# A hand-written order of steps and a table of due times set anew in an attention-then-gated-MLP kernel

## The chip, the cores and the metric

The kernel runs on one core of one Trainium2 chip. The metric is the device time of one execution in microseconds (us). Three runs of the kernel before are shown; an execution taken with the hardware profiler is a further one, and all rows of the trace come from that one.

## The reference

Attention over q, k, v of shape (4 batches, 8 heads, 768 positions, 64) feeds a gated MLP over 3072 tokens. Heads 0, 2 and 6 ("retrieval") see every earlier position; the other five ("streaming") see the first 4 positions and a window of 64.

```python
scores = scale * np.matmul(q, k.transpose(0, 1, 3, 2))
full_mask = causal                                  # retrieval heads
stream_mask = causal & (is_sink | in_win)           # the others
...
a = np.exp(scores - max) / sum
x = np.matmul(a, v)            # -> (3072, 512): a token's 8 heads side by side
h = x @ w_in                   # 512 x 2048
g = h * (1.0 / (1.0 + np.exp(-beta * h)))
out = (g @ w_out).astype(np.float32)                # 2048 x 512
```

## The kernel before

The 3072 tokens are eight chunks of 384 (a batch and one half of its sequence). A chunk has four units, each a pair of heads p and p + 4, so unit u belongs to chunk u // 4. The steps of a unit:

- casts to bf16 of q (`cq`) and k (`ck`), line 286, from a loaded f32 tile `s`; T: six 128 x 128 transposes on TensorE (PE, L371) and two copies out of PSUM, into `KT` (L373) and `QTD` (L377);
- S ("sinks", L354/L355; for one unit of a chunk also `QX`/`KX`, L350/L351): small copies that put the first four keys beside each block; V ("values", L292, L305/L306): v cast into `VX`, and its first rows beside each block in `VO`;
- Q: scores (L473 adds masks, L492 multiplies; L911 for the later chunks) and the exponential on ScalarE (ACT; L500, later L915); P: probabilities times v (L522) and the division (L525, L527); X: transposing the result into `xT` (L554, L556).

The MLP has two kinds of PE step. G1, written m or 1 in the lists below, is four 128 x 128 by 384-column matmuls with `w_in` (L588), a tanh on ACT (L591) and the gate on VectorE (DVE, L594). G2, written s or 2, is four 512-column matmuls with `w_out` (L630); each fourth is followed by an eviction `osb` and a store of 128 tokens (L640). Each chunk needs 16 G1 and 12 G2.

Every engine runs its instructions strictly in the order in which the program issues them (the schedule is manual), and so do the queues that issue transfers: SP for most loads, stores and DMA transposes, the queue of GpSimd (POOL) for `w_in`, `w_out` and the rows of chunks 3 to 7 (L318), ACT for a few. The order is therefore the whole of the tuning, and three tables write it out:

- `RAMP`: a list of tokens for chunks 0 and 1. `cq4p` casts q of unit 4 on POOL (d: DVE, a: ACT). `L10`, `Lv0p` load q/k of chunk 1 or v of chunk 0; a final p or d makes that engine first clear a few columns of the target, and the transfer waits for that. `T4aa` transposes unit 4 with both copies on ACT. `h` clears one column of `w_in_sb` on DVE, `W0` to `W3` load quarters of `w_in` (two transfers each; a G1 with index 0 to 3 needs W0, and so on), `O` loads `w_out` in four transfers. `o0` sets columns of ones, `B` prepares beta, `A1` loads the last third of v of chunk 1.
- `POST`: the tail of that list, with the remaining 24 G1 of chunks 0 and 1, the loads of chunk 2 (`L20` stands in RAMP, `L21d` and `Lv2d` here), its casts `C8`, `C9`, mask copies M, the transfers r of six rows of chunk 3, the transposes T8, T9 and the first four G2 (s).
- `SEQ`: one string for each of 16 groups of scores of chunks 2 to 7, saying which G1, G2 and halves of P (p, q) follow the group; the letters a, b, c are G1 or G2 with another PSUM bank. Beside it stand calls such as `rows_at(at(84), ...)`, `transposes_at`, `v_at`, `sinks_values`: they give a time on the planner's own clock, a running sum of fixed costs per step, at which a transfer or copy is put into its engine's order.

Of the kernel before, what the change touches and what calls it, by code (L numbers as in the profile page):

```python
# [17 lines left out]
def kernel(  # L18
# [14 lines left out]
    B, H, S, D = q.shape  # L33
# [53 lines left out]
    def later(delay, fn):  # L87

        todo = [fn]

        def once():
            if todo:
                todo.pop()()
        heapq.heappush(heap, (clock[0] + delay, count[0], once))
        count[0] += 1
        return once
# [18 lines left out]
    st_u = {}  # L115
# [172 lines left out]
    def cast_v(u, copy=None):  # L288
        b, h2, p = units[u]
        c = u // NPAIR  # L290
        copy = copy or (nc.vector.tensor_copy if 8 <= u < 16 else nc.gpsimd.tensor_copy)
        copy(out=VX[b % 2, p][:, h2 * HT:(h2 + 1) * HT, :, 0:D], in_=staged["v", c][:, :, p:H:NPAIR, :])  # L292

    def values(u, copy=None):

        b, h2, p = units[u]
        ka, kz = (1, 2) if h2 == 0 else (2, 5)
        n = kz - ka
        st_u.setdefault(u, {})["values"] = lambda: None
        cast_v(u, copy)  # L300
        if not streams[p]:
            return
        vx, vo = VX[b % 2, p], VO[b % 2, p]
        h0 = streams[p][0]
        nc.gpsimd.tensor_copy(out=vo[:, ka - 1:kz - 1, :, 0:D], in_=vx[:, ka:kz, h0:2, 0:D])  # L305
        nc.gpsimd.tensor_copy(out=vo[0:n_sink_i, ka - 1:kz - 1, :, 0:D],  # L306
                              in_=vx[0:n_sink_i, 0:1, h0:2, 0:D].to_broadcast([n_sink_i, n, 2 - h0, D]))

    def pos(b, hh):
        return hh ^ (b == B - 1)  # L310

    def load_rows(c):

        b, h2 = chunks[c]

        def one(name, src, t, hh):
            r, w = h2 * HALF + t * 128, pos(b, hh) * D
            nc.gpsimd.dma_start(out=ROWS[c % 2, name][:, t].rearrange("p (a w) -> p a w", a=NPAIR)[:, :, w:w + D],  # L318
                                in_=src[b, hh * NPAIR:(hh + 1) * NPAIR, r:r + 128, :].rearrange("h p d -> p h d"))
        return [lambda n=n, src=src, t=t, hh=hh: one(n, src, t, hh) for n, src in (("k", k), ("q", q)) for t in range(HT) for hh in range(2)]  # L320
# [19 lines left out]
    def sinks_of(u, eng=None):  # L340

        b, h2, p = units[u]
        ka, kz = (1, 2) if h2 == 0 else (2, 5)
        n = kz - ka
        st_u[u]["sinks"] = lambda: None
        if not streams[p]:
            return
        if lent(u):
            here, there = half(pos(b, 0)), half(1 - pos(b, 0))
            nc.gpsimd.tensor_copy(out=QX[u // NPAIR % 2][there, :], in_=st_u[u]["QT"][here, :])  # L350
            nc.gpsimd.tensor_copy(out=KX[b % 2][there, :], in_=KT[b % 2, p][here, 0:128])  # L351
        kt, ko = KT[b % 2, p], KO[b % 2, p]
        eng = eng or (nc.vector if u in (9, 11) else nc.gpsimd)
        eng.tensor_copy(out=ko[:, ka - 1:kz - 1, :], in_=kt[:, ka * 128:kz * 128].rearrange("p (a j) -> p a j", a=n))  # L354
        eng.tensor_copy(out=ko[:, ka - 1:kz - 1, 0:n_sink_i],  # L355
                              in_=kt[:, None, 0:n_sink_i].to_broadcast([128, n, n_sink_i]))
# [299 lines left out]
    h = FO // 2  # L656
# [74 lines left out]
        cast(u, "q")  # L731

    RAMP = """
    cq0p Lv0p ck0d cq1a L10 ck1p T0dd L11p S0p o0 ck2p Q0.m T1da@23 S1d cq2p cq3d Q0 ck3d
    T2ad Q1 T3da B S3d S2p Q2 V0d h W0 V2d P0 Lv1p Q3@6350 V1d V3d cq4p ck4a
    P2 ck5p X0d P1 P3 T4aa S4d cq5d o1 A1 X1a Q4.m Q4 X2d T5da X3d@7 ck6d S5p
    Q5@1603 cq6p W1 m ck7d T6da cq7p m T7da S6d S7d L20p W2 V4d Q6@6102 V6d V5d V7d
    W3 O m P4 Q7@6105 m X4a P5 P7 P6 m X5a m X7a m X6d m
    """

    fills = {}
# [44 lines left out]
        ramp(x)  # L786
    spare[0] = 1
    POST = """
    L21d m M m m m m m R m M m m m Lv2d M m m m m m r m m
    M m m C9 m m C8 m m m s r r T8aa s r r s T9aa s r  # L790
    """
    masks, rows3 = masks_late(1), []

# [36 lines left out]
    def event(kind, delay, fn, behind=()):  # L830

        when = max([clock[0] + delay] + [last_at.get(x, 0.0) + 1 for x in (kind, *behind)])
        last_at[kind] = when
        return later(when - clock[0], fn)

    def rows_at(at, some, gap=1000):
        for i, f in enumerate(some):
            event("rows", at + gap * i, f)

    def transposes_at(at, c, names=("k", "q"), gap=1300):  # L840
        for i, f in enumerate(transposes_dma(c, names)):
            f = event("transposes", at + gap * i, f, ("rows",))
            for u in range(c * NPAIR, (c + 1) * NPAIR):
                st_u[u].setdefault("load", []).append((f, last_at["transposes"]))

    def v_at(at, c, tiles):
        for i in tiles:
            event("v", at + 500 * i, lambda i=i: load_v(c, tiles=[i]))

    def sinks_values(u, at1, at2):  # L850
        s = st_u.setdefault(u, {})
        s["sinks"] = event("sinks", at1, lambda: sinks_of(u), ("transposes",))
        s["values"] = event("values", at2, lambda: values(u), ("v",))

    rows4 = load_rows(4)
# [112 lines left out]
                special[0] = None  # L968

    fresh, late_x = [10, 11], [10, 11]  # L970
    SEQ = ["2cTcTc", "2cqppcq", "2c2ppcppX2Xb1111a", "b22112c", "22c2", "pq121q11p111pp21pp", "ccc2cb12c", "211p1pcq1p1p1p1a2pp11ba", "bc2cca1b121b2", "pp2b211p1p21pp211p1pcc", "abc212c2b2c", "211b222bc", "pq1a1p21p1111pcp1q2p22", "2cb112c1b1a1b12", "2121b12211", "pp22qcpcc", "qpqp2a222c"]
    PVS = {1: [8, 9], 2: [10, 11], 5: [14, 12, 13, 15], 7: [18, 16, 17, 19], 9: [22, 20, 21, 23], 12: [26, 24, 25, 27], 15: [30, 28]}

    def at(us):
        return 1000.0 * us - clock[0]

    for gi in range(ng):
        pvs = PVS.get(gi, [])
        if gi == 0:
            rows_at(0, rows3)  # L980
            transposes_at(800, 3, ("k",), 0)
        if gi == 1:
            st_u[8]["values"]()
            st_u[9]["values"]()
            st_u[10]["values"] = later(1800, lambda: values(10))
            st_u[11]["values"] = later(8000, lambda: values(11))
            rows_at(6600, rows4[0:6], 300)
        if gi == 2:
            rows_at(4300, rows4[6:9], 300)
            transposes_at(500, 3, ("q",), 0)  # L990
            for u in range(12, 16):
                st_u.setdefault(u, {})['sinks'] = event('sinks', 7400, lambda u=u: sinks_of(u), ('transposes',))
        if gi == 3:
            clock[0] = max(clock[0], 75000.0)
            rows_at(at(67), rows4[9:], 1500)
            transposes_at(at(74.5), 4, ("k",))
            transposes_at(at(77.5), 4, ("q",))
            for i, f in enumerate(masks_late(0)):
                later(at(69 + i), f)
        if gi == 4:  # L1000
            v_at(at(83), 4, range(3))
            rows_at(at(84), load_rows(5))
        if gi == 6:
            for i, u in enumerate((18, 16, 17, 19)):
                sinks_values(u, at(87), at(109.5) + 2600 * i)
            transposes_at(at(98), 5, gap=1800)
        if gi == 7:
            v_at(at(103.5), 5, range(3))
            for i, u in enumerate((22, 20, 21, 23)):
                sinks_values(u, at(106.5), at(121) + 800 * i)  # L1010
            rows_at(at(118.5), load_rows(6), 300)
        if gi == 8:
            transposes_at(at(114), 6)
        if gi == 9:
            v_at(at(126), 6, range(3))
            for i, u in enumerate((26, 24, 25, 27)):
                sinks_values(u, at(102.5), at(155) + 3200 * i)
            rows_at(at(143.5), load_rows(7), 700)
        if gi == 10:
            transposes_at(at(147.5), 7)  # L1020
        if gi == 12:
            v_at(at(151), 7, range(3))
            for i, u in enumerate((30, 28, 29, 31)):
                sinks_values(u, at(163), at(150.5) + 1500 * i)
        if gi == 3:
            v_at(0, 3, range(3))
        if gi == 4:
            for i, u in enumerate((14, 12, 13, 15)):
                st_u[u]['values'] = event('values', 0 + 2600 * i, lambda u=u: values(u), ('v',))
        cycle(gi, SEQ[gi], pvs)  # L1030
    cycle(None, SEQ[ng], [u for u in order if last_in[u] == ng - 1])
    while True:
        m = next_m()
# [39 lines left out]
```

## Time and profile before

| | us |
|---|---|
| three runs | 226.93, 229.57, 319.99; median 229.57 |
| profiled execution, its own time | 226.46 |
| its span, first to last instruction | 224.7 |
| PE busy | 216.2 (96%) |
| PE idle in the span | 8.5 |

The profile page gives the busy time of each engine, the span in 40 slices, the chain of work that ended last, and the costliest groups of instructions. Where the text speaks of the timeline it means the instructions of one engine in order of time: start, duration, engine, line, what is written and read, and in brackets how long the engine had been idle and what released it. "issue to landing" is the time of a transfer from its issuing instruction to its data being there.

### The profile page before, as it was taken

The page shows a single profiled execution, that of the slowest core. Times are in us where ns is not written, and L with a number is a line of the kernel's source. Part 1 is how long each engine was busy: PE and PEld are TensorE (multiplying, and loading weights), DVE is VectorE, ACT ScalarE, POOL GpSimd, SP SyncE. Part 2 cuts the span into 40 slices and gives each one's busy share as a digit, 9 for nine tenths or more (in the row PEclk, how much of TensorE's full clock was granted, in tenths as well). Part 3 has the DMA queues.
Part 4 walks back from the last instruction along what each step waited for, and adds up shares of the span by engine and source line. Part 5 has one row for each costly group of instructions (what it writes and reads, how often), then busy time and mean ns, then how long its engine had stood idle before and what let it go on. Part 6 is the DMA issues. An engine that isn't in the chain of part 4 may idle for free.

```text
span 224.7 us, 5312 instructions
## 1 busy us (share of the span) xinstructions
PE 216.2 (96%) x1951; PEld 125.7 (56%) x1951; DVE 140.4 (62%) x364; ACT 154.2 (69%) x308; POOL 101.3 (45%) x227
## 2 busy tenths in 40 slices
PE   7787999999999999999999999999999999999994
PEld 2465766555655557545655565456655556546554
DVE  4776898966877648747957763354963566508700
ACT  2778988869756879467795857675938888238621
POOL 6375766019855848909992089800454000000000
PEclk9999999999999999999999999999999999999999
DMA  6999999999999999997995599917892101321012
GB/s 184 260 290 209 184 231 224 223 178 178 172 160 162 211 102 210 164 186 166 170 158 102 101 207 112 168 64 91 191 96 65 47 3 47 85 82 47 4 47 93
DMA packets 96730, 31.88 MB, mean 142 GB/s; under 512 B 83120, under 2 KB 93760, under 8 KB 96704
## 3 DMA queue, kind: packets, MB, share of 16 engines
q1 hardware_dynamic: 58288, 22.16, 49.1%
q0 software_dynamic: 35968, 8.13, 47.0%
q10 hardware_dynamic: 2448, 1.25, 2.1%
q8 instruction: 15, 0.25, 0.5%
q14 instruction: 11, 0.09, 0.1%
HBM read 27.27 MB, written 6.29 MB: 149 GB/s over the span
## 4 chain that ended last, share of the span: by engine, by line
PE 86%; DMA 8%; DVE 2%; POOL 1%; ACT 1%; issue 0%; ACTq 0%; SPq 0%; DVEq 0%
PE mm L588 37%; PE tp L630 35%; PE po L522 6%; PE sp L911 5%; DMA w_in_sb<-in_moe_w_in_dram 3%; DMA vs<-in_v_dram 3%; DMA s<-in_q_dram 2%; PE tp L615 2%; PE tp L371 1%; DVE es L438 1%; DVE KT L373 0%; PE tp L554 0%; POOL VO L305 0%; PE sp L492 0%; POOL w_in_sb L161 0%
## 5 line engine op out<-in xcount | busy, mean ns | idle before, releaser
L588 PE MATMUL mm<-xT,w_in_sb 128*128 128x384 bf16 x512 | 90.7, 326 | 0.9 <-DMA w_in_sb<-in_moe_w_in_dram 0.8
L594 DVE SCALAR_TENSOR_TENSOR gT<-th,mm 128x384 bf16<-128x384 f32 x128 | 68.4, 551 | 33.0 <-ACT th L591 27.5
L630 PE MATMUL tp<-w_out_sb,gT 128*128 128x512 bf16 x368 | 87.5, 379 | 0.0
L591 ACT ACTIVATE th<-mm,beta_h 128x384 f32<-128x384 f32 x128 | 73.5, 593 | 15.5 <-PE mm L588 10.4
L588 PEld LDWEIGHTS <-w_in_sb 128*128 128x128 bf16 x512 | 48.3, 98 | 33.6 <-issue 1.1
L915 ACT ACTIVATE es<-sp 128x512 bf16<-128x512 f32 (+1 forms) x104 | 49.4, 590 | 8.8 <-PE sp L911 8.8
L630 PEld LDWEIGHTS <-gT 128*128 128x128 bf16 x368 | 34.0, 98 | 35.7 <-DVE gT L594 0.3
L637 ACT ACTIVATE osb<-tp 128x512 f32<-128x512 f32 x20 | 12.0, 598 | 31.3 <-PE tp L630 27.7
L438 DVE TENSOR_TENSOR es<-es,Mh 128x512 bf16<-128x512 bf16 (+3 forms) x62 | 20.2, 366 | 7.7 <-ACT es L915 7.4
L318 POOL DMA_DIRECT2D s<-in_k_dram x30 | 22.4, 760 | 1.8 <-DMA w_out_sb<-in_moe_w_out_dram 1.7
L522 PEld LDWEIGHTS <-es 128*128 128x128 bf16 x472 | 19.2, 97 | 7.0 <-issue 1.2
L318 POOL DMA_DIRECT2D s<-in_q_dram x30 | 22.5, 771 | 0.6 <-issue 0.4
L522 PE MATMUL po<-VX,es 128*128 128x65 bf16 x392 | 20.6, 193 | 0.3 <-DVE w_in_sb L757 0.3
L350 POOL COPY QX<-QTD 64x384 bf16<-64x384 bf16 x4 | 2.0, 504 | 37.9 <-DMA QTD<-s 27.4
L527 DVE TENSOR_TENSOR x<-po,rec 128x384 bf16<-128x384 f32 x32 | 17.8, 558 | 1.3 <-DVE rec L525 0.2
L305 POOL COPY VO<-VX 128x128 bf16<-128x128 bf16 (+3 forms) x24 | 10.1, 419 | 13.0 <-DVE VX L292 7.8
L438 DVE TENSOR_TENSOR es<-es,Mc 128x384 bf16<-128x384 bf16 (+2 forms) x26 | 7.5, 296 | 10.5 <-ACT es L915 10.3
L911 PE MATMUL sp<-QTD,KT 64*128 64x128 bf16 (+2 forms) x245 | 13.9, 230 | 0.0
L500 ACT ACTIVATE es<-sp 128x384 bf16<-128x384 f32 (+1 forms) x32 | 12.0, 462 | 2.7 <-PE sp L492 2.5
L911 PEld LDWEIGHTS <-KT 64*128 64x128 bf16 x245 | 10.2, 94 | 4.7 <-issue 3.8
L354 POOL COPY KO<-KT 128x384 bf16<-128x384 bf16 (+1 forms) x18 | 7.4, 413 | 8.1 <-DMA KT<-s 5.6
L525 DVE RECIPROCAL rec<-po 128x6 f32<-128x6 f32 x32 | 6.1, 192 | 7.9 <-PE po L522 7.7
(79 smaller groups left out, 150.1 us busy)
## 6 DMA issues: line engine op xcount, KB each, us to landing
vs<-in_v_dram SPq DMA_DIRECT2D x23, 256.0 KB, 5.0
out_dram<-osb SPq DMA_DIRECT2D x23, 256.0 KB, 2.3
s<-in_k_dram SPq DMA_DIRECT2D x12, 192.0 KB, 4.8
w_in_sb<-in_moe_w_in_dram POOLq DMA_DIRECT2D x8, 256.0 KB, 7.3
w_out_sb<-in_moe_w_out_dram POOLq DMA_DIRECT2D x4, 512.0 KB, 15.8
s<-in_k_dram POOLq DMA_DIRECT2D x30, 64.0 KB, 5.1
s<-in_q_dram POOLq DMA_DIRECT2D x30, 64.0 KB, 5.0
s<-in_q_dram SPq DMA_DIRECT2D x8, 192.0 KB, 7.6
```

What stands on the lines that cost most here:

```text
L318: nc.gpsimd.dma_start(out=ROWS[c % 2, name][:, t].rearrange("p (a w) -> p a w", a=NPAIR)[:, :, w:w + D], in_=src[b, hh * NPAIR:(hh + 1) * ...
L438: nc.vector.tensor_mul(e, e, m)
L500: nc.scalar.activation(out=es[:, 0:w], in_=got[f][:, 0:w], func=ACTF.Exp, scale=scale)
L522: nc.tensor.matmul(po[:, qi, hh, :], e, val, start=(j == 0), stop=(j == len(lst) - 1))
L527: nc.vector.tensor_mul(x, po[:, :, :, 0:D], rec.to_broadcast([128, HT, 2, D]))
L588: nc.tensor.matmul(hp[:, 0:HALF], w_in_sb[:, mo, fi * 128:(fi + 1) * 128], xT[c][:, mo, :], start=(mo == 0), stop=(mo == MO - 1))
L591: nc.scalar.activation(out=th, in_=hp[:, 0:HALF], func=ACTF.Tanh, scale=beta_h[:, fi:fi + 1])
L594: nc.vector.scalar_tensor_tensor(out=gTs[c][:, fi, :], in0=th, scalar=1.0, in1=hp[:, 0:HALF], op0=ALU.add, op1=ALU.mult)
L630: nc.tensor.matmul(op, gTs[c][:, fi, ns * 128:(ns + 1) * 128], w_out_sb[:, fi, :], start=(fi == 0), stop=(fi == FO - 1))
L637: nc.scalar.activation(out=osb, in_=op, func=ACTF.Copy, scale=0.5)
L911: nc.tensor.matmul(sp[:, a * 128:z * 128], lhs[half(h)], rhs[half(h), q0 * 128:(q0 + z - a) * 128], start=True, stop=True)
L915: nc.scalar.activation(out=es[:, 0:w], in_=sp[:, 0:w], func=ACTF.Exp, scale=scale)
```

## The change

RAMP, POST and SEQ are reordered and most of the due times behind them are changed; no function, no tile size and no arithmetic changes. PE, ACT, DVE, POOL and the SP queue run the same work in another order, except that a few casts and copies change engine: `cq4` from POOL to DVE, `cq5` from DVE to ACT, `ck7` from DVE to POOL, the copy of X1 from ACT to DVE and that of X2 from DVE to ACT.

```diff
     RAMP = """
-    cq0p Lv0p ck0d cq1a L10 ck1p T0dd L11p S0p o0 ck2p Q0.m T1da@23 S1d cq2p cq3d Q0 ck3d
-    T2ad Q1 T3da B S3d S2p Q2 V0d h W0 V2d P0 Lv1p Q3@6350 V1d V3d cq4p ck4a
-    P2 ck5p X0d P1 P3 T4aa S4d cq5d o1 A1 X1a Q4.m Q4 X2d T5da X3d@7 ck6d S5p
-    Q5@1603 cq6p W1 m ck7d T6da cq7p m T7da S6d S7d L20p W2 V4d Q6@6102 V6d V5d V7d
-    W3 O m P4 Q7@6105 m X4a P5 P7 P6 m X5a m X7a m X6d m
+    Lv0p cq0p L10 cq1a o0 ck0d L11p ck1p T0dd S0p Q0.m T1da@23 ck2p S1d cq2p cq3d ck3d Q0
+    T2ad Q1 T3da h S2p B S3d Q2 V0d W0 V2d P0 Lv1p cq4d V1d Q3@6350 V3d ck4a
+    ck5p P2 X0d P1 cq5a P3 X2a T4aa S4d A1 o1 X1d Q4.m Q4 T5da cq6p ck7p X3d@7
+    S5p Q5@1603 ck6d W1 m T6da cq7p m T7da S6p L20p S7d W2 V4d V7d Q6@6102 V6d V5d
+    W3 O m P4 Q7@6105 m X4a P5 m P7 P6 m X5a m X7a X6d m
     """
...
     POST = """
-    L21d m M m m m m m R m M m m m Lv2d M m m m m m r m m
-    M m m C9 m m C8 m m m s r r T8aa s r r s T9aa s r
+    m m m L21d m Lv2d m m m m M m m m M R M m r m r m m m
+    m r m C8 T8aa m m r m m m m r M C9 s s T9aa r s s
     """
...
-    SEQ = ["2cTcTc", "2cqppcq", "2c2ppcppX2Xb1111a", "b22112c", "22c2", "pq121q11p111pp21pp", "ccc2cb12c", "211p1pcq1p1p1p1a2pp11ba", "bc2cca1b121b2", "pp2b211p1p21pp211p1pcc", "abc212c2b2c", "211b222bc", "pq1a1p21p1111pcp1q2p22", "2cb112c1b1a1b12", "2121b12211", "pp22qcpcc", "qpqp2a222c"]
+    SEQ = ["22TcTc", "2cqpqpc", "2c2ppcpqX2Xb1111a", "b2c1122", "2cc", "pqc11q211111qpp21pp", "2c22c21bc", "2111pp1cqp1p1p211pp11ba", "bcccca1b121b2", "pp2b12p112p21p1p1q1cq2", "abc221c2b22", "211b2c2bc", "pq11p2a1p11cp1q1q12p2c", "2cb12c11ba11b12", "2111b2c1c1", "apq2q2pc2", "qppp22c222"]
...
-            transposes_at(800, 3, ("k",), 0)
+            transposes_at(300, 3, ("k",), 0)
-            rows_at(4300, rows4[6:9], 300)
-            transposes_at(500, 3, ("q",), 0)
+            rows_at(1800, rows4[6:9], 500)
+            transposes_at(300, 3, ("q",), 0)
...
-            transposes_at(at(77.5), 4, ("q",))
+            transposes_at(at(80.5), 4, ("q",))
-            rows_at(at(84), load_rows(5))
+            rows_at(at(82.5), load_rows(5))
-                sinks_values(u, at(87), at(109.5) + 2600 * i)
-            transposes_at(at(98), 5, gap=1800)
+                sinks_values(u, at(86.5), at(115.5) + 2100 * i)
+            transposes_at(at(99.5), 5, gap=1800)
...
-            transposes_at(at(147.5), 7)
+            transposes_at(at(149), 7)
-            v_at(at(151), 7, range(3))
+            v_at(at(153.5), 7, range(3))
-                sinks_values(u, at(163), at(150.5) + 1500 * i)
+                sinks_values(u, at(162), at(150.5) + 2600 * i)
-                st_u[u]['values'] = event('values', 0 + 2600 * i, lambda u=u: values(u), ('v',))
+                st_u[u]['values'] = event('values', 0 + 300 * i, lambda u=u: values(u), ('v',))
```

In the built program, some moves show that the lists don't tell. The sinks of chunk 7 (QX, KX, KO on POOL), which stood before most of its values, stand behind all of them. On SP, the store of one `osb` moves from before the three `KT` transposes of chunk 7 to between the second and the third, and the first v transfer of chunk 5 moves ahead of that chunk's three `QTD` transposes.

More of the change, by code (lines that the diff above doesn't have):

```diff
@@ L984 @@
             st_u[9]["values"]()
-            st_u[10]["values"] = later(1800, lambda: values(10))
+            st_u[10]["values"] = later(500, lambda: values(10))
             st_u[11]["values"] = later(8000, lambda: values(11))
@@ L988 @@
         if gi == 2:
-            rows_at(4300, rows4[6:9], 300)
-            transposes_at(500, 3, ("q",), 0)
+            rows_at(1800, rows4[6:9], 500)
+            transposes_at(300, 3, ("q",), 0)
             for u in range(12, 16):
-                st_u.setdefault(u, {})['sinks'] = event('sinks', 7400, lambda u=u: sinks_of(u), ('transposes',))
+                st_u.setdefault(u, {})['sinks'] = event('sinks', 3600, lambda u=u: sinks_of(u), ('transposes',))
         if gi == 3:
             clock[0] = max(clock[0], 75000.0)
-            rows_at(at(67), rows4[9:], 1500)
+            rows_at(at(67), rows4[9:], 3000)
             transposes_at(at(74.5), 4, ("k",))
-            transposes_at(at(77.5), 4, ("q",))
+            transposes_at(at(80.5), 4, ("q",))
             for i, f in enumerate(masks_late(0)):
@@ L1001 @@
             v_at(at(83), 4, range(3))
-            rows_at(at(84), load_rows(5))
+            rows_at(at(82.5), load_rows(5))
         if gi == 6:
             for i, u in enumerate((18, 16, 17, 19)):
-                sinks_values(u, at(87), at(109.5) + 2600 * i)
-            transposes_at(at(98), 5, gap=1800)
+                sinks_values(u, at(86.5), at(115.5) + 2100 * i)
+            transposes_at(at(99.5), 5, gap=1800)
         if gi == 7:
-            v_at(at(103.5), 5, range(3))
+            v_at(at(104.5), 5, range(3))
             for i, u in enumerate((22, 20, 21, 23)):
-                sinks_values(u, at(106.5), at(121) + 800 * i)
-            rows_at(at(118.5), load_rows(6), 300)
+                sinks_values(u, at(107.5), at(116) + 300 * i)
+            rows_at(at(119.5), load_rows(6), 300)
         if gi == 8:
-            transposes_at(at(114), 6)
+            transposes_at(at(113.5), 6)
         if gi == 9:
-            v_at(at(126), 6, range(3))
+            v_at(at(127.5), 6, range(3))
             for i, u in enumerate((26, 24, 25, 27)):
-                sinks_values(u, at(102.5), at(155) + 3200 * i)
-            rows_at(at(143.5), load_rows(7), 700)
+                sinks_values(u, at(105.5), at(156.5) + 1300 * i)
+            rows_at(at(139.5), load_rows(7), 300)
         if gi == 10:
-            transposes_at(at(147.5), 7)
+            transposes_at(at(149), 7)
         if gi == 12:
-            v_at(at(151), 7, range(3))
+            v_at(at(153.5), 7, range(3))
             for i, u in enumerate((30, 28, 29, 31)):
-                sinks_values(u, at(163), at(150.5) + 1500 * i)
+                sinks_values(u, at(162), at(150.5) + 2600 * i)
         if gi == 3:
```

## Prediction

> **What bounds the kernel now.** I read the page first.
>
> ```profile
> PE 216.2 (96%) x1951; PEld 125.7 (56%) x1951; DVE 140.4 (62%) x364; ACT 154.2 (69%) x308; POOL 101.3 (45%) x227
> ```
>
> PE is busy for all but 8.5 of the span's 224.7 us, and the change adds and removes no PE instruction. So the question is where these 8.5 us lie, which the busy times by stretch answer (columns: stretch, its length, then PE busy with its count, weight loads, DVE, ACT, POOL).
>
> ```profile
> 1.30:22.00 20.70, 16.73 (x192) 9.78 (x193) 14.04 (x44) 14.30 (x35) 12.18 (x50) 1.00 1.12 253
> 22.00:31.15 9.15, 9.05 (x123) 6.46 (x121) 7.79 (x22) 8.09 (x20) 7.58 (x18) 1.00 1.11 202
> 31.15:48.00 16.85, 16.85 (x104) 10.07 (x103) 15.45 (x37) 14.84 (x26) 4.36 (x7) 1.00 1.21 216
> 75.00:190.00 115.00, 114.98 (x1032) 65.64 (x1031) 70.39 (x177) 83.11 (x164) 57.04 (x114) 1.00 1.02 126
> 221.90:224.70 2.80, 0.00 (x0) 0.00 (x0) 0.00 (x0) 0.23 (x1) 0.00 (x0) 1.00 0.16 47
> ```
>
> Before 22 us PE idles 20.70 - 16.73 = 3.97 us; from there to 31 us 0.10; in the 115 us from 75 to 190 0.02. The end, 2.8 us, is the last eviction and store, which the change does not touch, and 1.3 us pass before the first instruction. The granted clock is 1.00 throughout. So there is nothing to win behind 31 us and at most 4.1 us ahead of it; behind 31 us every new wait is a loss. The chain of waits says what set the start:
>
> ```profile
> 5.79 0.43 SPq L151
> ...
> 12.50 0.32 POOL VO L305
> ...
> 13.86 7.39 DMA w_in_sb<-in_moe_w_in_dram
> 21.25 0.14 issue
> 21.39 0.81 PE mm L588 x4
> ```
>
> The second of three v transfers of chunk 0 is issued at 5.79; when v is there it is cast on DVE and copied on POOL (12.50); behind that copy W0 is issued, its second half lands at 13.86 + 7.39 = 21.25, and the first G1 starts at 21.39. The PE timeline shows what PE did meanwhile, and that it then waited:
>
> ```profile
> 20.37 0.23 PE L492 MATMUL sp<-QTD,KT 64*128 64x128 bf16 x2
> 21.39 0.81 PE L588 MATMUL mm<-xT,w_in_sb 128*128 128x384 bf16 x4 [0.79 <-DMA w_in_sb<-in_moe_w_in_dram]
> ```
>
> 0.79 us is thus the wait that an earlier W0 can remove, while everything PE has left before it (up to the scores Q5, ending at 20.6) isn't slower.
>
> **The change, part by part.** *Lv0p to the front.* The rows of POOL, then those of DVE:
>
> ```profile
> 4.65 0.50 POOL L286 CAST qkb<-s 128x384 bf16<-128x384 f32 x1 [0.20 <-DMA s<-in_q_dram]
> 5.10 0.11 POOL L148 MEMSET vs<- 128x3 f32 x1
> ```
>
> ```profile
> 12.07 0.64 DVE L292 CAST VX<-vs 128x384 bf16<-128x384 f32 x2 [0.52 <-DMA vs<-in_v_dram]
> 12.38 0.06 DVE L757 MEMSET w_in_sb<- 128x1 bf16 x1
> ...
> 13.63 0.56 DVE L527 TENSOR_TENSOR x<-po,rec 128x384 bf16<-128x384 f32 x1
> 14.11 0.83 DVE L292 CAST VX<-vs 128x384 bf16<-128x384 f32 x2
> ```
>
> The clearing of `vs` at 5.10 no longer stands behind the cast cq0, so the first of three v transfers is issued up to 0.5 us earlier. But the second is issued at 5.79, by the chain as an earlier load lands, which the change leaves alone, and the last decides. Bounds: 0 (the second holds) to 0.5 us earlier (all three move); I take 0, as the chain's row shows the second one waiting. *h ahead of V0:* the VO copy at 12.50 starts when h ends (12.38 + 0.06); without h between, when V0's cast ends, about 12.07 + 0.64/2 = 12.39. Gain 0.05: W0 lands at 21.2.
>
> *cq4 on DVE.* The cast takes 0.55 us (quoted below) between x of unit 0, ending at 14.2, and V1, V3 at 14.11, pushing these and what follows back by 0.5. V1 feeds P1 and P3; their cover, POOL's VO copies, ends about when PE needs them, so PE reaches T4 some 0.2 us later (an estimate from these rows), which the next step's longer delay contains. *X2 before T4, and cq5 and X2's copy on ACT.* The rows of ACT:
>
> ```profile
> 15.50 0.54 ACT L286 CAST qkb<-s 128x384 bf16<-128x384 f32 x1
> 16.57 0.48 ACT L373 COPY KT<-tp 128x384 bf16<-128x384 bf16 x1 [0.53 <-PE tp L371]
> ...
> 18.19 1.53 ACT L500 ACTIVATE es<-sp 128x384 bf16<-128x384 f32 x4 [0.24 <-PE sp L492]
> 19.58 0.51 ACT L377 COPY QTD<-tp 128x384 bf16<-128x384 bf16 x1
> ```
>
> ACT had 0.53 us idle before T4's copy at 16.57. Now cq5 (another 0.54, from 16.04 to 16.55) and X2's copy (0.48, to 17.05) stand there, so T4's copies start about 0.5 later, Q4's exponentials at 18.7 instead of 18.19, and T5's copy, on which Q5 waits, at 20.1 instead of 19.58. Q5 then ends at 21.1 instead of 20.6. What covers this is the 0.79 us wait for W0; X2's three transposes, taken earlier, fill PE while it waits for T4's copies. So the first G1 starts at the later of 21.2 (W0) and 21.1 (Q5): 0.1 to 0.2 us earlier than 21.39, and the wait shrinks to 0.1. Were ACT's lag 0.8 us, the first G1 would be later than before by what exceeds it. *The rest of RAMP* (ck7 on POOL while it idled, V7 before V6, S6, which copies nothing, one m between P5 and P7) moves work within the stretch 22 to 31.15, where PE idles 0.10 us: 0.
>
> *POST.* T8 moves from behind the first G2 into the run of G1, C9 out of it.
>
> ```profile
> 48.42 0.34 PE tp L371 x6
> ```
>
> ```profile
> 48.63 0.48 ACT L373 COPY KT<-tp 128x384 bf16<-128x384 bf16 x1 [0.45 <-PE tp L371]
> 49.00 0.48 ACT L377 COPY QTD<-tp 128x384 bf16<-128x384 bf16 x1
> ```
>
> In that run, 31.15 to 48.00, ACT is busy 14.84 of 16.85 us and PE all of it. T8 brings 0.85 us of ACT work (48.63 to 49.48) against 0.34 of PE: ACT falls 0.5 us behind, which the free banks of `mm` may hide. Bounds 0 and 0.5; I take 0.1, as DVE, which sheds the cast of C9 (0.55), was at 15.45 of 16.85 there without stopping PE. *Lv2d and L21d.* A G1 takes 0.65 us (the 104 matmuls of that stretch are 26 G1 in 16.85 us). v of chunk 2 stands six G1 earlier in the list, 3.9 us, and L21 three later, 2 us; beside them runs the last `w_out` transfer:
>
> ```profile
> w_out_sb<-in_moe_w_out_dram POOLq DMA_DIRECT2D x1, 512.0 KB, 19.9
> ```
>
> ```profile
> 27.88 3.01 POOL L165 DMA_DIRECT2D w_out_sb<-in_moe_w_out_dram  x4
> ```
>
> ```profile
> 50.66 1.03 PE L630 MATMUL tp<-w_out_sb,gT 128*128 128x512 bf16 x4
> ```
>
> The fourth is issued at 27.88 + 3 x 0.75 = 30.1 and lands 19.9 later, at 50.0; the G2 that reads it runs at 50.66. Cover 0.65 us. In that stretch SP's queue has loads outstanding anyway, so I take 0; if not, below.
>
> *SEQ and due times.* The same G1 and G2 stand between the scores in each group to within one step, so they come where they came. What changes is how early the small copies are ready. The case that loses most cover is chunk 7; two stretches of POOL, its sinks and the last of its values, and the scores that read them:
>
> ```profile
> 159.90:162.90 3.00, 3.00 (x28) 1.91 (x27) 2.78 (x8) 2.49 (x6) 2.73 (x9) 1.00 1.06 246
> 166.60:171.60 5.00, 5.00 (x38) 2.54 (x37) 0.69 (x2) 3.33 (x8) 4.59 (x10) 1.00 0.33 92
> ```
>
> ```profile
> 180.14 0.22 PE L911 MATMUL sp<-QX,KX 64*128 64x128 bf16 x1
> ```
>
> Chunk 7's sinks ran in the first stretch (nine instructions, 2.73 us busy in 3.00). Now they stand behind the values, which end at 171.6: 171.6 + 3.0 = 174.6, with 180.14 - 174.6 = 5.5 us of cover. Charged 0; the 0.02 us of the long stretch bounds a gain, nothing bounds a loss.
>
> Sum against the profiled execution, 226.46: -0.15 + 0.1 = -0.05, so **226.4**. The median of the three runs, 229.57, is 3.1 us above that execution and the lowest run 0.5; two of four executions lie within 0.5 us, so I forecast on the profiled one.
>
> One rule speaks against the change.
>
> ```profile
> L286 POOL CAST qkb<-s x10: 499/504/537, 4.7 to 34.0; 128x384 bf16<-128x384 f32 x10
> ```
>
> ```profile
> L286 DVE CAST qkb<-s x6: 542/548/553, 4.3 to 20.3; 128x384 bf16<-128x384 f32 x6
> ```
>
> The DVE cast now falls at 14.1 to 14.7, over W0's second issue (13.86 to 14.5). If one blocked the other, W0 would land 0.55 later, at 21.8, and the first G1 start 0.4 later than before: 226.46 + 0.4 + 0.1 = 227.0. The POOL casts, some beside DVE's, spread over 38 ns, which speaks against it. The Trainium skill, SBUF — State Buffer, section "SBUF: two separate sides", has such a rule: an f32 copy on DVE inside SBUF can take the port pair that GpSimd needs to write its transfers' descriptors, and the later one waits for the whole instruction. By it the sum would be 227.0; the trace, as far as these casts show, doesn't agree.
>
> **The rivals.** (1) *The start gains more:* v lands 0.5 earlier and ACT keeps up; PE loses all of the 0.79 wait. 226.46 - 0.8 = 225.7. For it: the earlier first v transfer. Against: the row at 5.79. (2) *DVE blocks POOL,* or T8's ACT work shows in full: 227.0, as above. (3) *w_out lands late.* If v of chunk 2, 3.9 us earlier on the other queue, takes half the engines for those 3.9 us, the fourth `w_out` lands 1.95 us later and the G2 at 50.66 waits 1.95 - 0.65 = 1.3: 226.46 + 1.3 = 227.8. For it: cover of 0.65 only. Against: SP's queue is loaded either way. The Trainium skill, DMA: Bandwidth & Descriptors, section "Queues, rings and completion order", says each engine alternates between the queues that have work, packet by packet; by that rule the half above is the share. (4) *Slower:* the v transfers of chunk 7 stand on SP behind the store now between its KT transposes; that store waits for its `osb`. If they slip by more than 5.5 us, sinks and PE at 180.14 slip by the excess; from 10 us on the kernel is 4.5 us slower, about 231. For it: nothing in the trace bounds that store. Against: its G2 moves by a step or two, under 1 us each. (5) *The change doesn't act at all* where it is meant to: PE's Q5 becomes the bound as W0 did; that is inside the forecast.
>
> **How the numbers follow.** Forecast, 226.4 ± 0.6 us, 0.54; (1) 0.14; (2) 0.08; (3) 0.08; (4) and the like in other groups 0.11; a gain over 4.5 us, which would need more than the 4.1 us of idle, so that instructions now stretched by waits would have to shorten too, 0.05. Two per cent, 4.5 us, is about what a measurement of this kernel can tell from no change. Only (4) is slower by that: faster 0.05, same 0.84, slower 0.11. The range: 225.3 takes in (1); above, the forecast, (2), (3) and the scatter by which the shown median lies 3 us over its own profiled execution: 229.4.
>
> **What would show it.** The wait of the first G1 for `w_in` falls from 0.79 to under 0.3 while that G1 still starts at 21.1 to 21.4; ACT's exponentials of Q4 start near 18.7; PE is again without gaps from 31 to 221.9 us. Wrong would be: an idle row over 0.5 us on PE behind 31 us, at the fourth G2 (rival 3) or at scores of chunk 7 (rival 4), or a first G1 before 20.8 (rival 1).

## The result and the profile after

| | before | after |
|---|---|---|
| median of 22 runs each, side by side | 227.06 | 228.00 |
| lowest | 225.89 | 227.08 |
| profiled execution, its own time | 226.46 | 228.09 |
| its span | 224.7 | 226.4 |

The ratio after to before is 1.0047, with a 95% interval of 1.0027 to 1.0067: the changed kernel is slower by about 1.07 us (0.0047 x 227.06). A few runs in which the chip was in a slower state are left out of it, so it differs a little from the ratio of the medians above. The loss is far inside two per cent, and the time lies in the range given; but it is a loss where a change of -0.05 us was forecast, and it can be told from none.

First, where along the span the loss arises. The chain of waits lists PE's work in order of time (start, duration, what); the scores at L911 and the last transposes at L615 stand in both kernels and serve as milestones. The kernel before:

```profile
51.68 0.66 PE sp L911 x13
...
125.00 0.67 PE sp L911 x20
...
147.27 0.82 PE sp L911 x19
...
218.28 3.55 PE tp L615 x48
```

The kernel after:

```profile
52.07 0.66 PE sp L911 x13
...
125.44 0.67 PE sp L911 x20
...
148.90 0.82 PE sp L911 x19
...
219.90 3.55 PE tp L615 x48
```

After minus before: 0.39 at the first scores of chunk 2, 0.44 at 125 us, 1.63 at 148.9, 1.62 at the end. So in these two executions there are two steps, about 0.4 us lost before 52 us and 1.2 us lost between 125 and 149, and everything else costs nothing that shows. The list of waits on PE (who waited for whom, us in total, times, longest) names the second at once, in the kernel after:

```profile
PE mm L588 <- DMA xT<-x: 1.0, 1, 1.0
```

That line is not in the list of before, while the wait of L588 for `w_in`, 0.8 us there, is gone. PE's timeline of the kernel after shows which G1 it is:

```profile
142.79 0.65 PE L588 MATMUL mm<-xT,w_in_sb 128*128 128x384 bf16 x3
144.47 0.32 PE L588 MATMUL mm<-xT,w_in_sb 128*128 128x384 bf16 x1 [1.03 <-DMA xT<-x]
```

In the kernel before, the same G1 runs without a gap:

```profile
141.49 0.81 PE L588 MATMUL mm<-xT,w_in_sb 128*128 128x384 bf16 x4
```

A G1 has four matmuls, one for each unit's slice of `xT`. This is the first G1 of chunk 5: in the kernel after three slices are there, the fourth, that of unit 23, is 1.03 us late. The SP queue tells why. Before:

```profile
133.06 5.01 SPq L538 DMA_TRANSPOSE xT<-x  x3
138.31 0.40 SPq L640 DMA_DIRECT2D out_dram<-osb  x1
```

After, with the row of ScalarE that the store waits for:

```profile
134.31 3.14 SPq L538 DMA_TRANSPOSE xT<-x  x2
138.75 0.36 SPq L640 DMA_DIRECT2D out_dram<-osb  x1
139.20 1.21 SPq L538 DMA_TRANSPOSE xT<-x  x1
```

```profile
138.13 0.60 ACT L637 ACTIVATE osb<-tp 128x512 f32<-128x512 f32 x1 [1.33 <-PE tp L630]
```

Before, the last transpose of the chunk stood ahead of the store. After, the store of an `osb` stands ahead of it, and the store waits for its eviction, which ends at 138.13 + 0.60 = 138.73. This swap is one more move on the SP queue beside the two that the section on the change names. The chain of waits walks the same way:

```profile
138.13 0.60 ACT osb L637
...
139.20 5.23 DMA xT<-x
...
144.47 0.32 PE mm L588
```

x of unit 23 was there at 138.09 (its division on DVE runs from 137.53 for 0.56), so the store held the transpose from 138.1 to 139.2, 1.1 us. The transpose takes 5.23 us to land, and PE pays 1.03 of it. (The new order also makes that x 1.2 us later than before, where it was there at 136.87, and the G1 1.3 us later; experiment 1 shows what this alone does.) In the kernel before there was hardly any cover to lose, cover being the time from the landing of the data to its being read. Its last transpose, on SP:

```profile
136.90 1.18 SPq L538 DMA_TRANSPOSE xT<-x  x1
```

It landed 5.0 us after its issue, at 141.9, and the fourth slice was read at about 142.0: a cover of about 0.1 us.

The first step, 0.4 us, lies in RAMP. PE's timeline there, after:

```profile
20.24 0.43 PE L473 MATMUL sp<-Ns,idb 128*128 128x384 bf16 x2 [0.26 <-ACT es L500]
...
21.17 0.81 PE L588 MATMUL mm<-xT,w_in_sb 128*128 128x384 bf16 x4
22.24 0.49 PE L371 MATMUL tp<-idb,qkb 128*128 128x128 bf16 x6 [0.26 <-ACT es L500]
```

The first G1 waits for nothing and starts 0.22 us earlier than before (21.39). But behind it T6, which needs the PSUM bank of Q5's scores, now waits for ACT's exponentials of Q5, which it didn't before, so the lead is lost: T6 comes 0.21 us later. A second new wait ends the stretch:

```profile
31.36 0.34 PE L554 MATMUL tp<-idb,x 128*128 128x128 bf16 x3 [0.24 <-DVE x L527]
31.53 0.65 PE L588 MATMUL mm<-xT,w_in_sb 128*128 128x384 bf16 x3
```

The rows of T6 and of the run of G1 in the kernel before, neither with a wait:

```profile
22.03 0.50 PE L371 MATMUL tp<-idb,qkb 128*128 128x128 bf16 x6
...
31.15 1.14 PE L588 MATMUL mm<-xT,w_in_sb 128*128 128x384 bf16 x6
```

The run of G1 starts at 31.53 against 31.15 before. X6 waits for the last division on DVE. DVE's timeline, after and then before, shows a gate (L594) that has come between the two last divisions (L527):

```profile
29.58 0.56 DVE L527 TENSOR_TENSOR x<-po,rec 128x384 bf16<-128x384 f32 x1
30.05 0.54 DVE L594 SCALAR_TENSOR_TENSOR gT<-th,mm 128x384 bf16<-128x384 f32 x1
...
30.74 0.56 DVE L527 TENSOR_TENSOR x<-po,rec 128x384 bf16<-128x384 f32 x1
```

```profile
29.38 0.56 DVE L527 TENSOR_TENSOR x<-po,rec 128x384 bf16<-128x384 f32 x1
...
30.08 0.56 DVE L527 TENSOR_TENSOR x<-po,rec 128x384 bf16<-128x384 f32 x1
```

It is the gate of the G1 that RAMP moved between P5 and P7; the division comes 0.66 us later.

### The profile page after: what moved, and what is told of

The parts are those of the page before. It is cut to its first block, busy times and chain, and to the rows that moved or that the text cites. A ratio compares the mean times of both kernels' runs of the same rounds, so it can differ in the third digit from the quotient of the medians.

```text
span 226.4 us, 5286 instructions
## 1 busy us (share of the span) xinstructions
PE 215.3 (95%) x1929; PEld 125.8 (56%) x1951; DVE 140.9 (62%) x363; ACT 154.1 (68%) x309; POOL 100.8 (45%) x227
## 3 DMA queue, kind: packets, MB, share of 16 engines
q1 hardware_dynamic: 58288, 22.16, 49.8%
## 4 chain that ended last, share of the span: by engine, by line
PE 82%; DMA 7%; DVE 4%; ACT 2%; issue 2%; POOL 1%; ACTq 0%; SPq 0%; DVEq 0%; POOLq 0%
PE mm L588 35%; PE tp L630 33%; PE po L522 6%; PE sp L911 5%; DMA vs<-in_v_dram 3%; DMA xT<-x 2%; DMA s<-in_q_dram 2%; PE tp L615 2%; ACT es L500 1%; DVE x L527 1%; PE tp L371 1%; POOL VO L305 1%; PE sp L492 1%; PE sp L473 1%; DVE gT L594 1%
## 5 line engine op out<-in xcount | busy, mean ns | idle before, releaser
L588 PE MATMUL mm<-xT,w_in_sb 128*128 128x384 bf16 x512 | 90.8, 326 | 1.2 <-DMA xT<-x 1.0
L594 DVE SCALAR_TENSOR_TENSOR gT<-th,mm 128x384 bf16<-128x384 f32 x128 | 68.4, 551 | 36.7 <-ACT th L591 31.0
L591 ACT ACTIVATE th<-mm,beta_h 128x384 f32<-128x384 f32 x128 | 73.4, 594 | 18.7 <-PE mm L588 13.7
L630 PE MATMUL tp<-w_out_sb,gT 128*128 128x512 bf16 x346 | 84.1, 379 | 1.4 <-issue 0.3
L588 PEld LDWEIGHTS <-w_in_sb 128*128 128x128 bf16 x512 | 48.2, 98 | 32.5 <-DVE x L527 0.5
L438 DVE TENSOR_TENSOR es<-es,Mh 128x512 bf16<-128x512 bf16 (+3 forms) x62 | 20.7, 374 | 6.2 <-ACT es L915 5.9
L527 DVE TENSOR_TENSOR x<-po,rec 128x384 bf16<-128x384 f32 x32 | 17.8, 557 | 1.1
L305 POOL COPY VO<-VX 128x128 bf16<-128x128 bf16 (+3 forms) x24 | 9.6, 399 | 15.5 <-DVE VX L292 14.8
L292 POOL CAST VX<-vs 128x384 bf16<-128x384 f32 x16 | 8.1, 526 | 18.2 <-DMA vs<-in_v_dram 18.2
L438 DVE TENSOR_TENSOR es<-es,Mc 128x384 bf16<-128x384 bf16 (+2 forms) x26 | 8.3, 324 | 11.3 <-ACT es L915 11.2
L911 PE MATMUL sp<-QTD,KT 64*128 64x128 bf16 (+2 forms) x245 | 13.9, 230 | 0.0
L911 PEld LDWEIGHTS <-KT 64*128 64x128 bf16 x245 | 10.2, 94 | 5.1 <-issue 4.6
```

Source lines behind the costliest of these rows:

```text
L438: nc.vector.tensor_mul(e, e, m)
L527: nc.vector.tensor_mul(x, po[:, :, :, 0:D], rec.to_broadcast([128, HT, 2, D]))
L588: nc.tensor.matmul(hp[:, 0:HALF], w_in_sb[:, mo, fi * 128:(fi + 1) * 128], xT[c][:, mo, :], start=(mo == 0), stop=(mo == MO - 1))
L591: nc.scalar.activation(out=th, in_=hp[:, 0:HALF], func=ACTF.Tanh, scale=beta_h[:, fi:fi + 1])
L594: nc.vector.scalar_tensor_tensor(out=gTs[c][:, fi, :], in0=th, scalar=1.0, in1=hp[:, 0:HALF], op0=ALU.add, op1=ALU.mult)
L630: nc.tensor.matmul(op, gTs[c][:, fi, ns * 128:(ns + 1) * 128], w_out_sb[:, fi, :], start=(fi == 0), stop=(fi == FO - 1))
```

## The experiments

The theory after reading the profile: the loss is the transpose behind the store (about 1.2 us in the profile) plus ACT's and DVE's lag in the new RAMP (about 0.4). The main rival: a loss in transfers that the profiled execution happens not to show, or in other parts of the order. Ten kernels ran, each with 6 to 12 timed runs beside the kernel before on the same chip; every ratio is to that. Experiments 1 to 4, 5 to 8, and 9 and 10 ran on three chips, and a ratio has an interval of about 0.2% to each side, so a difference of two ratios is uncertain by some 0.3%, 0.6 us. The position of the scores of chunk 2 is that of the first instruction at L911 in the chain of waits, 51.68 before and 52.07 after.

**1. Transpose first.** The kernel after, with the fourth transpose of chunk 5 put into SP's order without delay, so that it stands ahead of the store:

```diff
-                        later(700, lambda: x_by_dma(u))
+                        later(0 if u == 23 else 700, lambda: x_by_dma(u))
```

> The changed kernel with one edit: the fourth xT transpose of chunk 5 is issued on SP ahead of the store that stood before it. If the store is what made it late (theory), it is issued at 138.1, when its x is ready, instead of 139.2, lands near 143.3, the wait of 1.03 us at the G1 that reads it falls under 0.2, the span falls by 1.0 to 1.2 us to about 225.3, and the ratio to the kernel before goes from 1.0047 to 1.000 +- 0.002. If the later place of the last P in the ninth string is what made it late (rival), the transpose still goes out after 138.7, the wait stays over 0.6 and the ratio over 1.003. If something later takes the place of the wait (second rival), the wait goes but the ratio stays over 1.003.

Measured: 226.91, ratio 1.0021 (1.0002 to 1.0040), span 225.1. SP and PE in this kernel:

```profile
133.86 5.35 SPq L538 DMA_TRANSPOSE xT<-x  x3
139.30 0.54 SPq L640 DMA_DIRECT2D out_dram<-osb  x1
```

```profile
142.71 0.81 PE L588 MATMUL mm<-xT,w_in_sb 128*128 128x384 bf16 x4
```

All four slices are read without a gap; the wait is gone, and the span is 1.3 us shorter than after's. Of the 0.47% some 0.26% are gone, and 0.21% are left: a little more than was expected, as the 0.4 us of RAMP had not been counted there. The transpose was issued at 138.03 and landed after 4.4 us, at 142.4; the fourth slice was read at 143.2. So the later x alone, the rival, left 0.8 us of cover: it is the store in front that made the wait.

**2. Store first, in the kernel before.** The opposite edit: the same transpose is delayed until it stands behind the store.

```diff
-                        later(700, lambda: x_by_dma(u))
+                        later(1800 if u == 23 else 700, lambda: x_by_dma(u))
```

> The kernel before with the reverse edit alone: the fourth xT transpose of chunk 5 goes behind the store that followed it. Theory: that store waits for its osb until 138.3, the transpose is issued at 138.75 instead of 136.9 and lands near 143.8; the G1 that reads it wanted it at 142.0: a wait of 1.8 us, ratio to before 1.008 (1.006 to 1.009). Rival (stores and transposes on SP pass without cost, the loss has another cause): no wait, ratio 1.000 +- 0.002.

Measured: 228.47, ratio 1.0079 (1.0055 to 1.0102), span 226.6. The SP queue and the G1 of this kernel:

```profile
138.07 0.36 SPq L640 DMA_DIRECT2D out_dram<-osb  x1
138.51 1.21 SPq L538 DMA_TRANSPOSE xT<-x  x1
```

```profile
143.84 0.32 PE L588 MATMUL mm<-xT,w_in_sb 128*128 128x384 bf16 x1 [1.94 <-DMA xT<-x]
```

One swap of two entries in one queue makes the kernel before slower than the whole change does. Here the G1 comes at 141.25, earlier than in the kernel after (142.79), so it waits longer, 1.94 us, and 0.0079 x 226.69 = 1.8 us of it show in the time; about as expected (1.8 us, 1.006 to 1.009). With the first experiment this settles the cause of the second step from both sides.

**3. Old RAMP and POST in the kernel after.**

> The changed kernel with RAMP and POST of before; SEQ and due times stay new. Theory: the 0.4 us by which the changed kernel reaches the scores of chunk 2 later comes from the new RAMP and goes with it, the 1.0 to 1.2 us at the transpose stay: first scores of chunk 2 at 51.7 instead of 52.07, ratio to before 1.005 +- 0.002, so 0.4 us under the changed kernel. Rival (the ramp's shift is recovered behind, as the transposes and casts of chunk 2 are then waited for): no difference from the changed kernel. If the new SEQ needs the new POST (second rival), new idle rows appear between 48 and 64 us and it is slower than the changed kernel.

Measured: 227.22, ratio 1.0025 (1.0004 to 1.0045), span 226.0. PE waits 1.36 us for `xT` at chunk 5, and the scores of chunk 2 come at 51.42, so the 0.4 us are gone and the other step stays. The ratio lies just under the 1.003 to 1.007 that were expected.

**4. New RAMP and POST in the kernel before.**

> The kernel before with RAMP and POST of the changed kernel; SEQ and due times stay old. Theory: only the ramp's 0.4 us: scores of chunk 2 at 52.05 instead of 51.68, no wait at the G1 of chunk 5, ratio 1.002 (1.000 to 1.003). Rival (new ramp and store interact: an earlier or later arrival decides the wait at the transpose): the wait of 1 us appears here too, ratio 1.005 or more.

Measured: 227.28, ratio 1.0019 (0.9999 to 1.0039), span 225.3; scores of chunk 2 at 52.13, no wait for `xT`. In PE's timeline of this kernel both waits of the new RAMP stand again:

```profile
22.30 0.49 PE L371 MATMUL tp<-idb,qkb 128*128 128x128 bf16 x6 [0.41 <-ACT es L500]
...
31.41 0.34 PE L554 MATMUL tp<-idb,x 128*128 128x128 bf16 x3 [0.25 <-DVE x L527]
```

The two halves add up: 0.19% (experiment 4) and 0.25% (experiment 3) make 0.44%, and the change costs 0.47%, each with 0.2% to both sides. The interval of the RAMP half alone touches 1, so by these times alone it isn't certain. The lowest runs speak for it: 226.66 here and 226.54 in experiment 1, with the new RAMP, against 225.91 for the kernel before beside them (29 runs). The next experiments look at it.

**5. ACT's load put back.** Experiment 1, with cq5, X1 and X2 at the place and on the engine that they had before.

```diff
-    ck5p P2 X0d P1 cq5a P3 X2a T4aa S4d A1 o1 X1d Q4.m Q4 T5da cq6p ck7p X3d@7
+    ck5p P2 X0d P1 P3 T4aa S4d cq5d A1 o1 X1a Q4.m Q4 X2d T5da cq6p ck7p X3d@7
```

> The changed kernel with the transpose first (as in the first experiment) and, in RAMP, X2, X1 and cq5 where and on the engines where they stood before. Theory: X2's copy and cq5 on ACT put T4's copies and the exponentials of Q4 and Q5 0.5 us back, and T6, whose PSUM bank Q5 holds, waits for them (0.41 us in the first experiment); with them back, exponentials of Q4 start at 18.1 instead of 18.65, T6's wait is under 0.1, scores of chunk 2 start 0.3 to 0.5 earlier, near 51.65 instead of 52.05, ratio to before 1.000 +- 0.002. Rival (w_in's landing again sets the pace): the wait moves to the first G1, which then starts no earlier than 21.0, T6 right behind it, and the gain is under 0.2.

Measured: 226.31, ratio 0.9989 (0.9972 to 1.0005), span 224.7, scores of chunk 2 at 51.66. PE's timeline:

```profile
21.18 0.81 PE L588 MATMUL mm<-xT,w_in_sb 128*128 128x384 bf16 x4 [0.64 <-DMA w_in_sb<-in_moe_w_in_dram]
21.82 0.50 PE L371 MATMUL tp<-idb,qkb 128*128 128x128 bf16 x6
22.16 0.81 PE L588 MATMUL mm<-xT,w_in_sb 128*128 128x384 bf16 x4
```

The first G1 starts when it did in the kernel after, at 21.18, though now it waits 0.64 us for `w_in` again; but T6 behind it waits for nobody, and the second G1 starts at 22.16 instead of 22.57. So the rival came in its first half, the wait at the first G1, and not in its second: the scores of chunk 2 come 0.39 us earlier than in experiment 1 (52.05). The two ratios (1.0021 there) differ by 0.3%, or 0.7 us, which the intervals allow to be anything from 0.1 to 0.6%. So taking back what cq5, X1 and X2 did together is enough to remove the RAMP step, and nothing that shows is left of the loss. X6's wait is still there (0.25 us); it uses up the 0.21 us by which the second G1 is ahead of the kernel before (22.37).

**6. The G1 between P5 and P7 put back.** Experiment 1, with that G1 behind X7 as before.

```diff
-    W3 O m P4 Q7@6105 m X4a P5 m P7 P6 m X5a m X7a X6d m
+    W3 O m P4 Q7@6105 m X4a P5 P7 P6 m X5a m X7a m X6d m
```

> The changed kernel with the transpose first and, in RAMP, only the G1 that moved between P5 and P7 put back behind X7. Theory: its gate stands on DVE ahead of the division of the last unit, so X6 waits for x (0.25 us in the first experiment); put back, that wait goes and scores of chunk 2 start 0.2 earlier, near 51.85. Rival (X6 waits because everything on DVE is late by ACT's lag): the wait stays and nothing moves.

Measured: 226.68, ratio 1.0031 (0.9998 to 1.0063). In the profile X6's wait is gone, T6's 0.42 us stays, and the scores of chunk 2 come 0.17 us earlier than in experiment 1. The times can't show 0.17 us (0.08%) with an interval of 0.65%; the price of this edit rests on the profile alone.

**7. Both.**

> The two last edits together. Theory: they add, scores of chunk 2 at 51.4 +- 0.15, span 224.5, ratio to before 0.999 to 1.000; what is left of the new RAMP (v's clearing first, h first, cq4 on DVE, ck7 on POOL) is worth 0 to 0.2 us to the good. Rival (what is left costs by itself, cq4 on DVE above all): scores of chunk 2 at 51.7 or later.

Measured: 226.15, ratio 1.0001 (0.9979 to 1.0023). The time is that of experiment 5, but the profiled execution (226.78, slower than its median) missed the mark: scores of chunk 2 at 52.03 and not 51.4. Its PE timeline has another new wait:

```profile
25.19 0.43 PE L522 MATMUL po<-VX,es 128*128 128x65 bf16 x9 [0.25 <-DVE VX L292]
```

and its chain of waits leads back to a transfer of v of chunk 1:

```profile
14.53 10.05 DMA vs<-in_v_dram
```

In this execution that v took 10 us, and P4 had to wait for its cast. Nothing in the two edits changes that transfer's place in its queue. But 51.7 or later was also the sign of the rival, that the rest of the new RAMP costs something by itself, so this profile doesn't refute it; the times speak against it (1.0001, lowest run 225.85).

**8. Only the front in the kernel before.** v of chunk 0 first, o0 and the second load of chunk 1 ahead of ck1, and `h` ahead of V0:

```diff
-    cq0p Lv0p ck0d cq1a L10 ck1p T0dd L11p S0p o0 ck2p Q0.m T1da@23 S1d cq2p cq3d Q0 ck3d
-    T2ad Q1 T3da B S3d S2p Q2 V0d h W0 V2d P0 Lv1p Q3@6350 V1d V3d cq4p ck4a
+    Lv0p cq0p L10 cq1a o0 ck0d L11p ck1p T0dd S0p ck2p Q0.m T1da@23 S1d cq2p cq3d Q0 ck3d
+    T2ad Q1 T3da h B S3d S2p Q2 V0d W0 V2d P0 Lv1p Q3@6350 V1d V3d cq4p ck4a
```

> The kernel before with only the first part of the new RAMP: v's clearing first on POOL, the ones and the clearing for the next load ahead of ck1, h ahead of V0. Theory: W0 is issued at 12.9 instead of 13.12 and lands 0.1 to 0.3 earlier; first G1 at 20.8 to 21.2, scores of chunk 2 at 51.2 to 51.5, ratio 0.999 +- 0.002: too little to tell from no change by time. Rival (the first v transfer, issued earlier, holds up q and k of units 2 and 3): T2 and T3 later than 7.9 and 10.2 and no gain at the first G1.

Measured: 226.15, ratio 0.9998 (0.9971 to 1.0026). PE's timeline:

```profile
20.56 0.82 PE L588 MATMUL mm<-xT,w_in_sb 128*128 128x384 bf16 x4
21.80 0.49 PE L371 MATMUL tp<-idb,qkb 128*128 128x128 bf16 x6 [0.41 <-ACT es L500]
```

The first G1 starts 0.83 us earlier than in the kernel before and waits for nothing. Little of that is the edit's: W0 was issued at 13.07 against 13.12, and not at 12.9 as expected, but its two transfers landed after 6.2 us (median) against 7.0. Yet the gain is 0.2 us at T6 (21.80 against 22.03) and none in the time: where `w_in` doesn't hold PE, ACT's exponentials do, 0.41 us of it at the next step.

**9. Old RAMP, new SEQ, transpose first.** The last cell of the square: experiment 3 with the edit of experiment 1.

> RAMP and POST of before, everything else as after, with the fourth xT transpose of chunk 5 ahead of the store: the last cell of the square of old and new RAMP by old and new SEQ. Theory (the whole loss is the transpose behind its store plus ACT's and DVE's lag in the new RAMP; the rest of SEQ and of the due times is worth nothing): no wait for xT at chunk 5, first scores of chunk 2 at 51.4 to 51.7, span 224.4 to 224.8, ratio to before 0.997 to 1.001. Rival A (the rest of SEQ costs something of its own): PE idle rows behind 52 us, ratio 1.002 or more. Rival B (SEQ gains once the two faults are out): ratio below 0.997.

Measured: 226.12, ratio 0.9989 (0.9969 to 1.0009). In its profile PE doesn't wait for `xT`, and no wait over 0.2 us stands behind 52 us. So SEQ and the due times, with the one transpose in its place, neither cost nor bring anything that shows, that is, more than 0.3%. The profiled execution was the slowest of its twelve runs, 227.37 with a span of 225.7, and missed the positions that were expected: scores of chunk 2 at 52.6. Its timeline says what was late in this execution, `w_in` at the first G1 and the v of chunk 1 behind `VO` (15.19 to 25.17 in its chain of waits, as late as in experiment 7):

```profile
21.96 0.81 PE L588 MATMUL mm<-xT,w_in_sb 128*128 128x384 bf16 x4 [1.32 <-DMA w_in_sb<-in_moe_w_in_dram]
...
26.44 0.19 PE L522 MATMUL po<-VO,es 128*128 128x65 bf16 x1 [0.23 <-POOL VO L306]
```

**10. The same with the front of experiment 8.**

> The kernel of the run before in this list, with v of chunk 0 loaded first and the clearing of w_in ahead of V0 as well, the only part of the new RAMP that shortens a wait. Theory: first G1 at 20.6 without a wait for w_in, T6 then waits 0.4 for ACT, scores of chunk 2 at 51.4, span 224.4, ratio 0.996 to 1.000: no gain beyond the noise, as ACT takes back what W0 gives. Rival (w_in's landing is what scatters the time from run to run, so that the runs close up and the median falls): ratio 0.994 to 0.997, spread of the runs under 0.5 us.

Measured: 226.19, ratio 0.9980 (0.9957 to 1.0003), runs from 225.90 to 226.70, span 224.3. No version ran that is faster than the kernel before beyond its interval; this one comes nearest. The first G1 starts at 20.85, still 0.39 us behind `w_in`, so the wait didn't vanish as expected, and the runs spread over 0.8 us where the rival asked for less than 0.5.

## Why the prediction was wrong

*The start, up to the first G1: right, step by step.* ACT's exponentials of Q4 were to start at 18.7, T5's copy at 20.1, the first G1 at 21.1 to 21.2 with its wait for `w_in` nearly gone. ACT's timeline of the kernel after:

```profile
18.65 1.53 ACT L500 ACTIVATE es<-sp 128x384 bf16<-128x384 f32 x4 [0.61 <-PE sp L492]
20.04 0.51 ACT L377 COPY QTD<-tp 128x384 bf16<-128x384 bf16 x1
```

and the G1 stands at 21.17 without a wait, bound by PE's own scores Q5, as rival 5 said; rival 1, a first G1 before 20.8, did not come. Two things in it are luck. W0 was issued 0.21 us earlier (12.91 against 13.12) where 0.05 had been charged. And the 21.39 of before is one execution: with the same RAMP the first G1 stood anywhere from 20.90 to 21.96 (last section), so that a gain of 0.15 us could not have been told from the scatter.

*The gain of 0.15 us, carried to the end, and "The rest of RAMP ...: 0": wrong, 0.4 us.* In the profiles the 0.22 us gained at the first G1 were 0.20 us lost at the second G1 (22.57 against 22.37, T6's wait) and 0.38 us lost at 31.53 (X6's wait, from the m between P5 and P7). The first of these steps followed ACT's lag to the first G1 and stopped there, as if a lag ended at the milestone for which it had been worked out. The wait for `w_in` had been covering ACT for T6 too; once PE no longer waited, ACT's exponentials of Q5 became the next bound. That PE idled only 0.10 us in that stretch bounded what could be gained there and said nothing of what could be lost; for SEQ the prediction said so itself, and for RAMP it took the same number for a reason to charge nothing.

*"So they come where they came", charged 0: the step that failed most, 1.2 us in the profile and 0.6 to 0.8 us by the times of experiments 1, 3 and 9.* It looked for the cover of the readers by groups of scores and checked one case, the sinks of chunk 7, with 5.5 us. The case with the least cover was another: `xT` of the last unit of a chunk, read about 0.1 us after it had landed. The prediction asked what is queued behind a waiting store once, in chunk 7 (rival 4), and not for the store that came ahead of a transpose of chunk 5 on the same queue. It named the right sign of it, an idle row over 0.5 us on PE behind 31 us, though at neither of the places that it had in mind; the row of 1.03 us is that. That the measured time still lies in the range is luck: its upper end, 229.4, was set for rivals 2 and 3 and for scatter, and none of these made the loss.

*POST, v and w_out of chunk 2 (rival 3): as forecast.* From 31.5 to 52 us the lag stays at 0.38 to 0.39 us, so T8's work on ACT cost nothing where 0.1 had been charged, and the fourth G2 after the last `w_out` had no wait.

*Rival 2, DVE's cast blocking POOL, did not come.* POOL's two issues of W0 after, and the casts of v on DVE behind cq4:

```profile
12.91 1.38 POOL L161 DMA_DIRECT2D w_in_sb<-in_moe_w_in_dram  x2
```

```profile
14.43 0.62 DVE L292 CAST VX<-vs 128x384 bf16<-128x384 f32 x2
```

DVE's cast cq4 ran from 13.97 to 14.51, over the end of the second issue (12.91 + 1.38 = 14.29). It took the 0.54 us of DVE's other casts of this kind, and the pair took 1.38 us in the kernel before as well. The rule cited from the Trainium skill, SBUF — State Buffer, section "SBUF: two separate sides", would have had one of the two wait for the other, as the prediction applied it; of these two neither did. But another cast did wait, in the kernel before. There the two casts of v stood in cq4's place, and the prediction shows their row, 14.11 for 0.83 us, where 0.62 to 0.64 us are usual. The first of them took 0.57 us and not 0.35, and it ended at 14.68, 0.18 us after W0's second issue (14.50). In all six profiles in which a cast of v starts during that issue (before and experiments 2, 3, 8, 9 and 10) it takes 0.49 to 0.57 us and ends 0.18 us after the issue; in the six in which cq4 stands between, it takes 0.35. By these rows DVE waits for POOL there, which agrees with the rule; why cq4 doesn't wait, no run shows. So cq4 pushed the casts of v back by only 0.1 us (they end at 15.05 against 14.94) where the prediction had 0.5.

*Rival 4, slower by the SP queue in chunk 7,* had the right mechanism, a store that holds what stands behind it, at the wrong place and with a price of 4.5 us instead of 1.0. In chunk 7 PE shows no new wait.

## What to carry to other kernels

When entries of an in-order queue are exchanged, look up for each the time at which its data is ready and the time at which its reader needs it, and start with the smallest cover: here one store ahead of one transpose, whose data had 0.1 us of cover in the kernel before, made about half of the loss by the times (0.25 of 0.47%) and three quarters of it in the profile (1.2 of 1.6 us). And when a change removes a wait, follow every engine that this wait was covering past the point where it ended; what was hidden behind a wait of 0.8 us came out at the next step. An idle share near zero bounds a gain, never a loss.

## What was not expected of the hardware

The same transfers, issued at the same place of the order, land at quite different times from one execution to the next. The list of transfers issued from 12 to 18 us (queue, count, KB each, median us from issue to landing), in the kernels of experiments 3 and 9 in turn, whose RAMP is the same:

```profile
w_in_sb<-in_moe_w_in_dram POOLq DMA_DIRECT2D x2, 256.0 KB, 6.4
...
vs<-in_v_dram SPq DMA_DIRECT2D x2, 256.0 KB, 7.6
```

```profile
w_in_sb<-in_moe_w_in_dram POOLq DMA_DIRECT2D x2, 256.0 KB, 7.5
...
vs<-in_v_dram SPq DMA_DIRECT2D x2, 256.0 KB, 9.1
```

With the RAMP of before, unchanged, the first G1 started at 20.90 (experiment 3), 21.00 (2), 21.39 (before) and 21.96 (9), and each time it waited for `w_in`. With the new RAMP it never waited: 20.98 to 21.17 in the four profiles that have cq5 and X2 on ACT. There the scores of chunk 2 come at 51.9 to 52.1, while the old RAMP has them at 51.3 to 51.7 in three profiles and at 52.6 in experiment 9. One could think that the change trades an early start for one that bears a late `w_in`; that is not shown, as in these four the two transfers took 6.0 to 6.9 us and never the 7.5 of experiment 9. Why the landings scatter stays open: no run varied anything that would tell.
